# Where the gated layer's lead runs beside the last expert item: token sums on VectorE, splits directly behind them, block loads and sums earlier

## The chip, the cores and the metric

One core of a Trainium2 chip runs the whole program. The metric is device time in microseconds (us) of one execution, the median of several runs.

## What is computed

Attention output (3072 tokens of width 512) goes through a mixture of eight experts with one expert per token, and then through a gated layer:

```python
# experts: x [3072, 512], w1 [8, 512, 1024], w2 [8, 1024, 512]
for e in range(E):
    xe = x[expert_idx == e]
    h = np.maximum(xe @ w1[e], 0.0)
    out[expert_idx == e] = gate_w[expert_idx == e, None] * (h @ w2[e])
# gated layer: w_gate, w_val [512, 1536], w_out [1536, 512]
gate = 1.0 / (1.0 + np.exp(-(x @ w_gate)))
val = x @ w_val
return (gate * val @ w_out).astype(np.float32)
```

All of it is in float32.

## The kernel before

A float32 product is made of three TensorE products of rounded parts: each operand is split into a high part (a rounded copy, made on ScalarE, ACT) and a low part (the operand less the high part, made on VectorE, DVE), and high by high, high by low and low by high are added in PSUM.

**The experts** (`ffn`, `Moe`) run over nine items, each a group of tokens of one expert. An item has eight steps f = 0 to 7, one for each 128 of the 1024 hidden columns. A step has two groups of 12 matmuls: `mm1(i, f)`, L1101, here called *hidden product f*, whose result ACT and DVE turn into `hh` (L1105) and `hl` (L1106); and `mm2(i, f)`, L1118, here *output product f*, which needs `hh`, `hl` and the weights of the second layer. In the program the order within step f is: weight splits (`wh` on ACT, L999; `wl` on DVE, L1004), weight loads (L990), hidden product f + 1, then for the last item (i = 8, 352 tokens) `m2.lead(f)`, and then output product f. Each pair of weights serves two steps: the first layer's pair for hidden products 4 and 5 is split in step 2, the second layer's pair for output products 4 and 5 in step 3.

**The gated layer** (`Gated`) runs over four chunks of 768 tokens. For a chunk it multiplies 2 x 2 blocks with seven products instead of eight, so both operands need four sums of blocks besides the four blocks. A token operand is built twice, for u = 0 and 1: `yfetch` loads four blocks of 128 x 384 from `yT` with three DMAs (L1231 to L1233) into a tile `raw`, `ysum` adds four blocks (L1240), and `ysplit` splits blocks 1 to 4 (z = 0, 1536 columns) and 5 to 7 (z = 1, 1152 columns) into the tiles `yo` (L1246 on ACT, L1247 on DVE). A weight operand s = 0 to 11 is built in the same way: `afetch` (L1254), `asum` (L1265), `asplit` (L1279 on ACT, L1280 on DVE, into `set`), and `astore` (L1268) writes the blocks and sums out for the later chunks. `raw` has two buffers, so the load of a block waits for the split that last read its buffer. The products of set s are `first(s)` (L1331, seven products of six matmuls each).

`lead(f)` puts the first chunk's token operand and the first sets beside the last item's steps. Its last act, in step 7, is to start `first(0)`: two products X and Y of six matmuls each, which TensorE (PE) takes ahead of output product 7. The item before stores its result to `yT` (L1129) at the start of the last item, and the first `yfetch` waits for that store.

The order of instructions on every engine is the order in which the program issues them; nothing reorders them. The line that matters in `ffn` is the step's body:

```python
        if n + 1 < len(steps):
            mm1(*steps[n + 1])
...
            m2.lead(f)
        mm2(i, f)
```

Of the kernel before, what the change touches and what calls it, by code (L numbers as in the profile page):

```python
# [14 lines left out]
ALU = mybir.AluOpType  # L15
# [42 lines left out]
NSET = 2 * NJ  # L58
# [168 lines left out]
def graph():  # L227
# [12 lines left out]
    for t in range(NTILE):  # L240
# [15 lines left out]
        for s in (2 * t, 2 * t + 1):  # L256
# [4 lines left out]
            for j in range(4):  # L261
                first = [("NS", WIN if t else 128, s % 2)] if t < 2 and j == 0 else []
                add(
                    ("TTR", s, j), [("QK", s)] + first, [("QK", s, j - 2)] if j >= 2 else (),
                    cost=0.318 if i else 0.21,
                )
                add(
                    ("EXP", s, j), [("TTR", s, j)] + ([("PT", s - 3, 1)] if s >= 3 and j == 0 else []),
                    cost=0.38 if i else 0.293,
                )  # L270
# [937 lines left out]
class Gated:  # L1208
# [25 lines left out]
            out=x[:, 2:4, :].rearrange("p b n -> p (b n)"), in_=self.g.yT[(u + 2) * 128 : (u + 3) * 128, cols]  # L1234
        )

    def ysum(self, c, u):
        x = self.yr[c, u]
        for o, a, b in ((4, 0, 1), (6, 3, 0), (5, 3, 4), (7, 2, 5)):
            self.tc.nc.gpsimd.tensor_tensor(x[:, o, :], x[:, a, :], x[:, b, :], op=ALU.subtract)  # L1240

    def ysplit(self, c, u, z):
        x = self.yr[c, u]
# [93 lines left out]
    def first(self, s):  # L1337

        nc = self.tc.nc
        j, m = divmod(s % NSET, 2)  # L1340
        V, A, G = nc.vector, nc.scalar, nc.gpsimd
        last = s % NSET == NSET - 1
        X, Y, Z, W = (self.psum(b, f"q{b}")[:, :CH] for b in ((2, 3, 0, 1) if m else (6, 7, 4, 5)))
        u2 = self.tm.tile([128, CH], F32, tag="u2", name="u2", bufs=2)
        c, r = divmod(s, NSET)
        more = c + 1 < NCH
        if c == 0 and r < NSET - 2:
            self.asum(s + 2)
        if more and r >= NSET - 2:
            self.ysum(c + 1, r - NSET + 2)  # L1350
        self.product(X, 1, 0, s)
        A.activation(u2, X, AF.Copy)  # L1352
        self.product(Y, 4, 4, s)
        V.tensor_tensor(u2, Y, u2, op=ALU.add)  # L1354
        yield
        if last:
            self.hsplit(0, 0, 2)
        else:
            self.asplit(s + 1, 0)
        self.product(Z, 5, 5, s)  # L1360
        at = lambda half, tok: self.h[:, 2 * j + half, tok * CH : tok * CH + CH]
        dst = (lambda half, tok: self.g.op.tile([128, CH], F32, tag="t", name="t", bufs=3)) if m else at
        d22 = dst(1, 1)
        V.tensor_tensor(d22, Z, u2, op=ALU.add)
        if last:
            self.hsplit(0, 2, 4)
        else:
            self.asplit(s + 1, 1)
        if r < NSET - 3:
            self.afetch(s + 3)  # L1370
        elif more and r < NSET - 1:
            self.yfetch(c + 1, r - NSET + 3)
        if c == 0 and r < NSET - 2:
            self.astore(s + 2)
        if c == 0:
            if r in (3, 5):
                self.ofetch((r - 3) // 2)
            if r in (6, 8):
                self.osplit((r - 6) // 2, G)
            if r in (8, 10):  # L1380
                self.ofetch((r - 8) // 2 + 2)
        elif r in (2, 4, 6):
            self.oload(c, r // 2 - 1)
        self.product(W, 3, 3, s)
        V.tensor_tensor(d22, W, d22, op=ALU.add)  # L1385

        def gate(d, half, tok):
            if m:
                (V if last else G).tensor_tensor(at(half, tok), at(half, tok), d, op=ALU.mult)  # L1389
            else:  # L1390
                A.activation(d, d, AF.Sigmoid)

        gate(d22, 1, 1)
        self.product(X, 2, 1, s, False)
        if m:
            V.tensor_tensor(at(0, 0), X, at(0, 0), op=ALU.mult)  # L1396
        else:
            A.activation(at(0, 0), X, AF.Sigmoid)
        self.product(Z, 0, 6, s, False)
        d21 = dst(1, 0)  # L1400
        V.tensor_tensor(d21, Z, u2, op=ALU.add)
        gate(d21, 1, 0)
        self.product(W, 6, 2, s, False)
        d12 = dst(0, 1)
        V.tensor_tensor(d12, W, u2, op=ALU.add)
        gate(d12, 0, 1)
        yield
# [75 lines left out]

    def lead(self, f):

        if f < 2:
            self.yfetch(0, f)
        if f in (1, 2):
            self.ysum(0, f - 1)
        if 2 <= f < 6:  # L1490
            self.ysplit(0, f // 2 - 1, f % 2)
        if f == 3:
            sg = self.tm.tile([128, 1], F32, name="sg")
            self.tc.nc.scalar.activation(sg, self.g.nval[:, 0:1], AF.Sigmoid)
        if f in (4, 6):
            self.afetch(f // 2 - 2)
            if f == 6:
                self.astore(0)
            self.asum(f // 2 - 2)
        if f == 7:  # L1500
            self.afetch(2)
            self.astore(1)
            self.now = self.first(0)
            next(self.now)

# [435 lines left out]
```

## Time and profile before

| | |
|---|---|
| time, median of 3 runs (lowest to highest) | 1102.04 us (1101.3 to 1102.1) |
| the profiled execution's own time | 1103.0 us |
| its span in the trace | 1101.1 us |
| PE busy | 1028.4 us, 93% of the span |
| DVE busy | 829.0 us, 75% |
| ACT busy | 566.3 us, 51% |
| GpSimd (POOL) busy | 441.5 us, 40% |
| mean granted TensorE clock | 0.974 |

Busy time of an engine is the time in which it executes an instruction; the rest it waits. The last expert item lies at about 507 to 547 us of the span, and the first chunk of the gated layer begins there. In the views, a time in brackets at the end of a row is how long the engine was idle before that instruction, with what ended the idle time.

### The profile page before, as it was taken

To read this page: it belongs to the slowest core of one execution; us is meant where nothing else is said; L and a number is where in the kernel's file an instruction comes from. 1 tells how busy PE (TensorE), PEld (TensorE's weight loads), DVE (VectorE), ACT (ScalarE), POOL (GpSimd) and SP (SyncE) were. 2 spreads that over 40 slices of the span, in tenths; PEclk is the share of its full clock that TensorE was granted. 3 is DMA by queue.
4 is the path that set the end of the run, shared out by engine and by line. 5 is a ranking of instruction groups with operands and counts; after the bars stand their busy time and mean duration, and the time that the engine had idled before them with its cause. 6 is when DMAs were issued, how large, how long until landed. Compare 5 with 4: busy or idle time off the path is not lost.

```text
span 1101.1 us, 21478 instructions
## 1 busy us (share of the span) xinstructions
PE 1028.4 (93%) x7983; PEld 981.2 (89%) x7983; DVE 829.0 (75%) x1663; ACT 566.3 (51%) x1027; POOL 441.5 (40%) x612
## 2 busy tenths in 40 slices
PE   6987978788999999999899998999999999999994
PEld 5776767688889999999899998999999999999994
DVE  6987869655679778975767699666986679766782
ACT  6998979533344444544544464444534436444440
POOL 7998879730221222130878713214122250222102
PEclk9999989798999999999999999999999999999997
DMA  9899986477598899987568758663465725656061
GB/s 193 193 189 182 194 182 125 119 167 259 178 278 276 276 308 293 303 274 203 187 227 286 271 189 316 227 243 126 156 233 190 249 91 187 234 199 224 18 230 62
DMA packets 176216, 229.45 MB, mean 208 GB/s; under 512 B 90243, under 2 KB 140038, under 8 KB 172518
## 3 DMA queue, kind: packets, MB, share of 16 engines
q1 hardware_dynamic: 170566, 214.04, 64.6%
q0 software_dynamic: 5008, 13.93, 3.7%
q8 instruction: 65, 1.06, 0.4%
q14 instruction: 49, 0.40, 0.1%
q10 hardware_dynamic: 528, 0.02, 0.0%
HBM read 163.13 MB, written 60.51 MB: 203 GB/s over the span
## 4 chain that ended last, share of the span: by engine, by line
PE 71%; POOL 10%; DVE 6%; DMA 5%; issue 4%; ACT 2%; SPq 1%; another core or an unknown queue 0%; POOLq 0%; DVEq 0%; ACTq 0%
PE q L1331 30%; PE p L1429 14%; PE hp L1101 12%; PE acc L1118 12%; DMA vb<-vv 2%; POOL pl L597 1%; POOL xr L640 1%; PE mxt L1036 1%; POOL vv L484 1%; POOL lst L735 1%; DMA wr<-in_moe_w_dram 1%; DVE set L1321 1%; POOL ph L590 1%; DMA x<-xd,idx 1%; PE ptp L573 1%
## 5 line engine op out<-in xcount | busy, mean ns | idle before, releaser
L1331 PE MATMUL q<-yo,set 128*128 128x384 f32 x2016 | 354.5, 337 | 3.1 <-ACT set L1279 1.3
L1331 PEld LDWEIGHTS q<-yo,set 128*128 128x128 f32 x2016 | 348.6, 188 | 8.0 <-DVE h L1385 2.3
L1429 PE MATMUL p<-wy,set 128*128 128x256 f32 x1458 | 175.4, 281 | 5.0 <-DVE set L1321 4.1
L1429 PEld LDWEIGHTS p<-wy,set 128*128 128x128 f32 x1458 | 173.7, 189 | 6.6 <-DVE set L1321 5.1
L1101 PE MATMUL hp<-xT,wh 128*128 128x256 f32 (+7 forms) x576 | 147.3, 341 | 0.1
L1389 POOL TENSOR_TENSOR h<-h,t 128x384 f32<-128x384 f32 x60 | 60.6, 1018 | 164.2 <-DVE t L1385 160.6
L1280 DVE TENSOR_TENSOR set<-raw,set 128x1024 fp32r<-128x1024 f32 x96 | 110.6, 1154 | 2.3 <-ACT set L1279 2.3
L1101 PEld LDWEIGHTS hp<-xT,wh 128*128 128x128 f32 x576 | 101.9, 192 | 3.2 <-ACT wh L999 0.4
L1101 PE MATMUL hp<-xT,wl 128*128 128x256 f32 (+7 forms) x288 | 96.8, 336 | 1.1 <-DVE wl L1004 1.1
L1118 PE MATMUL acc<-hl,wh 128*128 128x256 f32 (+7 forms) x288 | 96.2, 334 | 0.4 <-DVE hl L1106 0.4
L1118 PE MATMUL acc<-hh,wh 128*128 128x256 f32 (+7 forms) x288 | 96.5, 335 | 0.0
L1118 PE MATMUL acc<-hh,wl 128*128 128x256 f32 (+7 forms) x288 | 96.1, 334 | 0.0
L1016 POOL DMA_INDIRECT x<-xd,idx x29 | 32.4, 1116 | 154.9 <-DMA idx<-lst 134.2
L1279 ACT ACTIVATE set<-raw 128x1024 fp32r<-128x1024 f32 x96 | 85.8, 944 | 15.3 <-PE p L1429 11.9
L1105 ACT ACTIVATE hh<-hp 128x256 fp32r<-128x256 f32 (+7 forms) x72 | 34.7, 482 | 113.3 <-PE hp L1101 110.2
L1004 DVE TENSOR_TENSOR wl<-wr,wh 128x1024 fp32r<-128x1024 f32 x64 | 80.9, 1266 | 13.2 <-ACT wh L999 11.8
L1352 ACT ACTIVATE u<-q 128x384 f32<-128x384 f32 x48 | 23.6, 492 | 122.1 <-PE q L1331 122.1
L1475 POOL DMA_INDIRECT out_dram<-o,idt x24 | 25.2, 1051 | 148.9 <-ACT set L1279 78.5
L1354 DVE TENSOR_TENSOR u<-q,u 128x384 f32<-128x384 f32 x48 | 26.8, 558 | 74.8 <-PE q L1331 73.3
L1320 ACT ACTIVATE set<-h 128x1152 fp32r<-128x1152 f32 (+1 forms) x60 | 62.8, 1098 | 37.7 <-DVE h L1396 16.4
L561 ACT ACTIVATE pp<-tt,mall 128x232 f32<-128x232 f32 (+1 forms) x192 | 79.8, 479 | 2.3 <-DVE mall L544 2.3
L1321 DVE TENSOR_TENSOR set<-h,set 128x1152 fp32r<-128x1152 f32 (+1 forms) x60 | 76.6, 1314 | 2.2 <-ACT set L1320 2.0
(204 smaller groups left out, 2142.7 us busy)
## 6 DMA issues: line engine op xcount, KB each, us to landing
wr<-in_moe_w_dram SPq DMA_DIRECT2D x64, 512.0 KB
raw<-us SPq DMA_DIRECT2D x36, 896.0 KB
wy<-wz SPq DMA_DIRECT2D x21, 1536.0 KB
us<-raw SPq DMA_DIRECT2D x12, 896.0 KB
wz<-wy SPq DMA_DIRECT2D x7, 1536.0 KB
kn<-in_k_dram SPq DMA_DIRECT2D x24, 256.0 KB
qn<-in_q_dram SPq DMA_DIRECT2D x24, 256.0 KB
vn<-in_v_dram SPq DMA_DIRECT2D x24, 256.0 KB
```

Source lines behind the costliest of these rows:

```text
L561: nc.scalar.activation(pp[s][:, j, 256 - w :], tt[s][:, j, :w], AF.Exp, bias=g.mall[:, t, h : h + 1], scale=-1.0)
L1004: self.tc.nc.vector.tensor_tensor(lo, self.raws.pop((z, p)), hi.bitcast(F32), op=ALU.subtract)
L1101: nc.tensor.matmul(bk, a[:, k, fs], b[:, k, :], start=(m == 0), stop=(m == 11))
L1105: nc.scalar.activation(hh, bk, AF.Relu)
L1118: nc.tensor.matmul(acc[i][dk], a[:, f % 2, d], b, start=(f == 0 and m == 0), stop=(f == NF - 1 and m == 2))
L1279: self.tc.nc.scalar.activation(h, x, AF.Copy)
L1280: self.tc.nc.vector.tensor_tensor(l, x, h.bitcast(F32), op=ALU.subtract)
L1320: self.tc.nc.scalar.activation(h, x, AF.Copy)
L1321: self.tc.nc.vector.tensor_tensor(l, x, h.bitcast(F32), op=ALU.subtract)
L1331: nc.tensor.matmul(bk, w[:, za, a, us], self.y[zy][:, y, u, :], start=(start and n == 0), stop=(n == 5), skip_group_check=not start,)
L1389: (V if last else G).tensor_tensor(at(half, tok), at(half, tok), d, op=ALU.mult)
L1429: nc.tensor.matmul(bks[t], w[:, za, j, 128 * t : 128 * t + 128], y[:, zy, j, :], start=(new and j == 0 and m == 0 and (end or t != 1)), st ...
```

## The change

The first chunk's token sums move from POOL to DVE; the sums of later chunks stay on POOL. Both token loads are issued in step 0 (before: steps 0 and 1). Steps 1 and 2 each do the sums of one half u and at once both of its splits (before: one split in each of steps 2 to 5). The loads and sums of sets 0 and 1 move from steps 4 and 6 to steps 3 and 4, and both stores to step 5 (before: steps 6 and 7).

```diff
-    def ysum(self, c, u):
+    def ysum(self, c, u, e):
         x = self.yr[c, u]
         for o, a, b in ((4, 0, 1), (6, 3, 0), (5, 3, 4), (7, 2, 5)):
-            self.tc.nc.gpsimd.tensor_tensor(x[:, o, :], x[:, a, :], x[:, b, :], op=ALU.subtract)
+            e.tensor_tensor(x[:, o, :], x[:, a, :], x[:, b, :], op=ALU.subtract)
...
         if more and r >= NSET - 2:
-            self.ysum(c + 1, r - NSET + 2)
+            self.ysum(c + 1, r - NSET + 2, G)
...
     def lead(self, f):
 
-        if f < 2:
-            self.yfetch(0, f)
+        if f == 0:
+            self.yfetch(0, 0)
+            self.yfetch(0, 1)
         if f in (1, 2):
-            self.ysum(0, f - 1)
-        if 2 <= f < 6:
-            self.ysplit(0, f // 2 - 1, f % 2)
+            self.ysum(0, f - 1, self.tc.nc.vector)
+            self.ysplit(0, f - 1, 0)
+            self.ysplit(0, f - 1, 1)
         if f == 3:
             sg = self.tm.tile([128, 1], F32, name="sg")
             self.tc.nc.scalar.activation(sg, self.g.nval[:, 0:1], AF.Sigmoid)
-        if f in (4, 6):
-            self.afetch(f // 2 - 2)
-            if f == 6:
-                self.astore(0)
-            self.asum(f // 2 - 2)
+        if f in (3, 4):
+            self.afetch(f - 3)
+            self.asum(f - 3)
+        if f == 5:
+            self.astore(0)
+            self.astore(1)
         if f == 7:
             self.afetch(2)
-            self.astore(1)
             self.now = self.first(0)
             next(self.now)
```

Its effect on the order, first on DVE, in steps 1 to 4 of the last item. `wl0` is the low part of first-layer weights, `wl1` of second-layer weights; `raw2_8773` is the token tile of u = 0 and `raw2_8816` (in the change `raw2_8777`) that of u = 1. Before:

```order
L1106 SCALAR_TENSOR_TENSOR hl_8813<-hp_8799,hh_8812 128x352
L1004 TENSOR_TENSOR wl0_8837<-wr0_8735,wh0_8836 128x1024
L1106 SCALAR_TENSOR_TENSOR hl_8856<-hp_8842,hh_8855 128x352
L1247 TENSOR_TENSOR yo1_8772<-raw2_8773,yo0_8771 128x4x384
L1004 TENSOR_TENSOR wl1_8878<-wr1_8797,wh1_8877 128x1024
L1106 SCALAR_TENSOR_TENSOR hl_8897<-hp_8883,hh_8896 128x352
L1247 TENSOR_TENSOR yo1_8772<-raw2_8773,yo0_8771 128x3x384
```

The same stretch on DVE in the change:

```order
L1106 SCALAR_TENSOR_TENSOR hl_8817<-hp_8803,hh_8816 128x352
L1240 TENSOR_TENSOR raw2_8773<-raw2_8773 128x384 x4
L1247 TENSOR_TENSOR yo1_8772<-raw2_8773,yo0_8771 128x4x384
L1247 TENSOR_TENSOR yo1_8772<-raw2_8773,yo0_8771 128x3x384
L1004 TENSOR_TENSOR wl0_8841<-wr0_8735,wh0_8840 128x1024
L1106 SCALAR_TENSOR_TENSOR hl_8860<-hp_8846,hh_8859 128x352
L1240 TENSOR_TENSOR raw2_8777<-raw2_8777 128x384 x4
L1247 TENSOR_TENSOR yo1_8772<-raw2_8777,yo0_8771 128x4x384
L1247 TENSOR_TENSOR yo1_8772<-raw2_8777,yo0_8771 128x3x384
L1004 TENSOR_TENSOR wl1_8884<-wr1_8801,wh1_8883 128x1024
L1106 SCALAR_TENSOR_TENSOR hl_8903<-hp_8889,hh_8902 128x352
```

The four sums and both splits of u = 0 now stand ahead of the weights `wl0` for hidden products 4 and 5 and of `hl` of step 3; those of u = 1 stand ahead of the weights `wl1` for output products 4 and 5 and of `hl` of step 4.

On the queue of loads and stores (SP), from the last item's step 0 on, as one piece of the difference:

```order
-L990 ISA
-L990 DMA wr_8797<-in_moe_w_dram 128x2x512
-L1231 DMA raw_8816<-yT 128x384
-L1232 DMA raw_8816<-yT 128x384
-L1233 DMA raw_8816<-yT 128x768
+L1231 DMA raw_8777<-yT 128x384
+L1232 DMA raw_8777<-yT 128x384
+L1233 DMA raw_8777<-yT 128x768
+L990 ISA
+L990 DMA wr_8801<-in_moe_w_dram 128x2x512
```

The loads of u = 1 pass one load of second-layer weights, the one for output products 4 and 5; the three loads of u = 0 stay where they were, ahead of both.

## Rows read from the trace of the kernel before

**Rows 1.** Chain of waits in time: start us, us, what; last expert item.
```profile
512.70 1.93 PE acc L1118 x12
...
519.63 6.17 DMA raw<-yT
```

**Rows 2.** PE in time, last item: start us, us, engine, line, op, [idle before].
```profile
522.23 0.48 PE L1101 MATMUL hp<-xT,wh 128*128 128x352 f32 x2
...
528.70 0.43 PE L1118 MATMUL acc<-hl,wh 128*128 128x352 f32 x1 [0.36 <-DVE hl L1106]
...
532.29 0.43 PE L1101 MATMUL hp<-xT,wl 128*128 128x352 f32 x1 [0.85 <-DVE wl L1004]
...
542.51 0.62 PE L1331 MATMUL q<-yo,set 128*128 128x384 f32 x2 [1.30 <-ACT set L1279]
543.87 0.96 PE L1331 MATMUL q<-yo,set 128*128 128x384 f32 x4 [0.74 <-DVE set L1280]
...
546.60 71.11 PE L1331 MATMUL q<-yo,set 128*128 128x384 f32 x396
```

**Rows 3.** POOL in time, last item.
```profile
520.57 1.02 POOL L1240 TENSOR_TENSOR raw<-raw 128x384 f32<-128x384 f32 x1 [29.92 <-PE hp L1101]
522.65 12.96 POOL L1240 TENSOR_TENSOR raw<-raw 128x384 f32<-128x384 f32 x7 [1.06 <-DMA raw<-yT]
535.57 6.01 POOL L1265 TENSOR_TENSOR raw<-raw 128x256 f32<-128x256 f32 x4
542.27 3.65 POOL L1265 TENSOR_TENSOR raw<-raw 128x256 f32<-128x256 f32 x4 [0.69 <-DMA raw<-up]
```

**Rows 4.** SP in time: issues of loads and stores, last item.
```profile
511.49 0.40 SPq L1129 DMA_DIRECT2D yT<-y  x1
...
516.05 1.49 SPq L1231 DMA_DIRECT2D raw<-yT  x1
...
530.31 8.59 SPq L1254 DMA_DIRECT2D raw<-up  x2
```

**Rows 5.** DVE in time, last item.
```profile
517.12 0.53 DVE L1106 SCALAR_TENSOR_TENSOR hl<-hp,hh 128x352 fp32r<-128x352 f32 x1 [1.71 <-ACT hh L1105]
518.85 1.22 DVE L1004 TENSOR_TENSOR wl<-wr,wh 128x1024 fp32r<-128x1024 f32 x1 [1.21 <-ACT wh L999]
...
524.21 2.04 DVE L1247 TENSOR_TENSOR yo<-raw,yo 128x1536 fp32r<-128x1536 f32 x1 [2.70 <-ACT yo L1246]
526.17 2.03 DVE L1004 TENSOR_TENSOR wl<-wr,wh 128x1024 fp32r<-128x1024 f32 x1
```

**Rows 6.** DVE groups by shape, 640 to 1100 us: xcount | busy us, mean ns.
```profile
L1247 DVE TENSOR_TENSOR yo<-raw,yo 128x1536 fp32r<-128x1536 f32 x6 | 10.5, 1748 | 0.0
...
L1247 DVE TENSOR_TENSOR yo<-raw,yo 128x1152 fp32r<-128x1152 f32 x6 | 8.1, 1348 | 0.0
...
L1389 DVE TENSOR_TENSOR h<-h,t 128x384 f32<-128x384 f32 x9 | 5.5, 608 | 0.3
```

**Rows 7.** ACT in time, last item.
```profile
522.68 1.49 ACT L1246 ACTIVATE yo<-raw 128x1536 fp32r<-128x1536 f32 x1 [1.73 <-DMA raw<-yT]
```

**Rows 8.** Stretches: from:to, length, busy PE, PEld, DVE, ACT, POOL, clock, DMA, GB/s.
```profile
546.60:635.20 88.60, 87.97 (x495) 84.79 (x494) 62.83 (x90) 39.05 (x63) 69.17 (x62) 1.00 0.76 267
...
952.60:1040.00 87.40, 87.40 (x507) 87.40 (x506) 58.77 (x93) 37.88 (x61) 18.25 (x18) 1.00 0.45 168
```

**Rows 9.** PE in time, end of the attention stage.
```profile
202.40 0.21 PE L614 MATMUL po<-vb,ph 128*128 128x65 f16 x1 [4.46 <-DMA vb<-vv]
```

**Rows 10.** Stretches about that wait, columns as in rows 8.
```profile
206.00:208.00 2.00, 2.00 (x15) 1.94 (x15) 2.00 (x7) 1.37 (x4) 2.00 (x3) 0.50 0.00 0
208.00:210.00 2.00, 1.20 (x25) 1.06 (x23) 2.00 (x2) 2.00 (x5) 1.92 (x2) 0.97 0.00 0
...
214.00:216.00 2.00, 1.96 (x11) 1.48 (x10) 1.65 (x6) 1.29 (x4) 1.83 (x5) 0.50 0.27 105
```

**Rows 11.** Chain of waits in time, first expert item at the half clock.
```profile
252.42 2.56 PE acc L1118 x12
```

## The prediction

> **What bounds the kernel now.** I read the page's busy shares first: TensorE is busy for 93% of the span, so only a change that alters TensorE's gaps can alter the time. Then I read the chain of waits through the last expert item. It runs over TensorE's groups of 12 matmuls, 1.93 us each [rows 1], leaves TensorE at the token load, follows the token and weight sums on POOL and the last split, and comes back to TensorE at 543.87 [rows 1 to 3]. TensorE in time shows what that costs. From the start of hidden product 4 (522.23) to the first product behind output product 7 (546.60) are 24.37 us [rows 2]. The work in it is nine groups of 12 matmuls, 9 x 1.93 = 17.37 us, and X and Y, twelve products of 384 columns at 87.40/507 = 0.172 us each [rows 8], 2.08 us: 19.45 us. **4.92 us are lost**, at four places: output product 4 waits for `hl`, hidden product 6 for `wl`, X and Y for the high and the low part of set 0 [rows 2]. The brackets there count idle time alone, 3.25 us; I go by starts. These 4.92 us are all that the change can win in this stretch. Behind it, the first chunk's products take 88.60 us and the last chunk's 87.40 [rows 8], so 1.2 us more lie there at most.
>
> **What the change does, step by step.** I set it on the clock of the trace before.
>
> 1. *The sums of u = 0 now wait on DVE.* DVE is through with `hl` of step 2 at 517.65 [rows 5], and its next instruction is the first sum. On POOL that sum began at 520.57 and the next one only at 522.65, when the third load had landed [rows 3]. The load can't come earlier: its issue at 516.05 stands behind the store of the item before, issued at 511.49 [rows 4], and the change alters nothing ahead of it. So DVE is held from 517.65 to 522.65. What is queued behind: both splits, the low weights for hidden products 4 and 5 (before at 518.85 [rows 5]) and `hl` of step 3.
>
> 2. *How long the block takes.* A sum of 128x384 on DVE lies between 0.53 us (the `hl` of 352 columns [rows 5]) and 1.02 us (the same sum on POOL [rows 3]); I take 0.61, DVE's operation of the same shape [rows 6]. Three sums are left at 522.65: 1.8 us, to 524.45. The low parts take 1.75 and 1.35 us [rows 6]; instructions in a row overlap a little, and I take 2.95 for both, to 527.4. With the weights' 1.22 [rows 5] this is 528.6. The high parts on ACT (1.49 for the larger [rows 7], about 1.2 for the smaller one, from 524.45) and the weights' high part behind them are done near 526.7, ahead of DVE.
>
> 3. *First new wait.* Hidden product 4 starts two matmuls at most (and those not before 526.7) and needs the low weights for its third, at 522.23 + 2 x 0.16 = 522.55. It gets them at 528.6: **6.05 us lost**, where nothing was lost before.
>
> 4. *The block of u = 1.* Its loads pass a load of weights on SP; they landed at 525.8 before [rows 1] and can land sooner, so nothing waits for them. The weights that they pass are not split before 532, so that costs nothing either. DVE does `hl` of step 3 to 529.05, four sums to 531.4, both low parts to 534.35, the low weights for output products 4 and 5 to 535.5 and `hl` of step 4 to 536.0. This is without POOL. But the first `raw` buffer is free at 527.4, so set 0 is loaded some 3 us earlier than the 530.31 of before [rows 4], and its four sums begin on POOL about 3.7 us behind the issue (the second of the pair of issues ended at 538.9 and its sums began at 542.27 [rows 3, 4]), at 531.1, for 3.65 to 6.0 us [rows 3]. Where POOL adds beside it, DVE's low part took 2.04 instead of 1.75 and the weights 2.03 instead of 1.22 [rows 5, 6]. The cost here lies between nothing and 1.5 us; I take 1.1, since three of these operations fall into the stretch, and `hl` of step 4 is done at 537.1.
>
> 5. *Second new wait.* TensorE, back at 528.6, has ten matmuls left of hidden product 4 (1.6 us) and two groups, so output product 4 would start its second matmul at 534.2. It gets `hl` at 537.15: **2.95 us lost**.
>
> 6. *What goes.* From there on everything has slack. The table load and the Sigmoid now stand behind `hh` of step 4 on ACT and put off the weights for hidden product 6 to 538.3, or 539.1 beside POOL, where they are needed at 539.2; this is what is late next. The sums of sets 0 and 1 end before 543, X is not before 546.6, and the last split of set 0 follows `hh` of step 7 to some 547.0, where Y needs it at 547.65. So the four waits of before go, 4.92 us.
>
> 7. *What costs nothing.* POOL has no other work until the sums of set 0. Both stores only wait on SP, ahead of nothing but the load of set 2, which waits for the split of set 0 in any case.
>
> **Sum:** 6.05 + 2.95 - 4.92 = **+4.1 us**. The profiled execution took 1103.0 us of its own (span 1101.1 and 1.9 around it), 1.0 above the median of 1102.04; so 1107.1 for such an execution and **1106.1 us** for the median.
>
> **The clock.** TensorE rests from 522.2 to 526.7. A rest of 4.46 us at the end of attention was followed by half the clock (1.2 of 2.4 GHz) until about 208, 5.7 us behind the restart at 202.40 [rows 9, 10]. If this comes here, the 34 matmuls up to output product 4 take 2.8 us longer, and it is reached at 537.0 instead of 534.2, still before `hl`. The second wait hides it, and the sum stays. This I expect.
>
> **The rivals.** A change can be told from no change here from about 0.2%, 2.2 us.
>
> *The clock stays low longer.* For: after 212 the profile shows half the clock although TensorE was 1.96 of 2.00 us busy [rows 10]. At half the clock a group of 256 columns takes 2.56 us [rows 11], so a matmul of 352 takes 2.56/12 x 352/256 = 0.293 us. From 528.6 the 34 matmuls then last until 538.6; if the clock is back only at 541, eight of output product 4 are done by then and four follow in 0.6 us: 541.6 instead of 538.9. That is +6.8 us, **1108.8**. Against: in rows 9 and 10 it was back after 5.7 us. By the Trainium skill (TensorE: Matmul & The Clock Gate, parts 1 and 4) sustained matmuls release the clock again and transposes count for less. By that rule the stretch after 212, where many instructions are transposes, says little of this one, and the sum stays at +4.1 against +6.8 by the row. No run here has shown yet which holds behind such a wait among products. The chance of this rival is 0.12.
>
> *POOL hardly collides, and the first chunk gains.* If set 0's sums fall beside DVE's waits, the 1.1 us go; if the sets' loads, now nearer to ready, spare the first chunk what it loses against the last one, 1.2 more go. This gives +1.8 us, **1103.9**, which counts as no change. For: POOL's sums beside TensorE's waits took only 3.65 us once [rows 3]. Against: the first chunk's loss recurs with its own stores and sums, which the change leaves. Chance 0.15.
>
> *Faster.* One place decides: the landing of the third load of u = 0. Each us that it comes sooner takes one off the first wait; the second wait moves with it. At 518.55 the sum is zero, and at 516.6 it is -2 us, **1100.1**. Against: the load was issued between 516.05 and 518.5 and first needs the store to land; nothing in the change speeds that up. Chance 0.05, general doubt about the order of the waits included.
>
> **How the numbers follow.** The forecast has 0.68: its own range goes from 1104.5 (no collision, sums a tenth of a us shorter) to 1107.7 (the largest collision and the slower sums). The whole range takes in the second rival and most of the first, 1103.2 to 1108.8. Slower by over 0.2% (above 1104.2): the forecast and the clock's rival, 0.80. Within 0.2%: the rival of the small loss, 0.15. Faster: 0.05.
>
> **What would show it.** Right: the four brackets of rows 2 are gone; TensorE waits 4 to 6 us at hidden product 4 for `wl` behind the token splits, then 1 to 3 us at output product 4 for `hl`; DVE sits idle before its first token sum until the third load; X and Y run without a wait, and the products behind output product 7 start near 550.7. Wrong: hidden product 4 starts on time, or the token loads land before 519; a granted clock below 1 beyond 536 would speak for the clock's rival; and if the first chunk's products took 87.4 us, for the small loss.

## The result and the profile after

| | before | after |
|---|---|---|
| median of 11 runs each, side by side (lowest to highest) | 1101.3 us (1096.42 to 1104.37) | 1106.91 us (1102.5 to 1113.33) |
| the profiled execution's own time | 1103.0 us | 1108.95 us |
| its span | 1101.1 us | 1107.0 us |
| PE busy | 1028.4 us | 1028.3 us |
| mean granted TensorE clock | 0.974 | 0.972 |

The ratio is 1.0055, with a 95% interval of 1.0032 to 1.0077: **slower, by 3.5 to 8.5 us**. The forecast was 1106.1 us, which is +4.1 on the earlier median of 1102.04; side by side the medians lie 5.6 us apart.

The executions of either kernel lie some 8 to 11 us apart, more than the effect, so two traces can't be compared by their spans. The changed kernel's trace already stands 3.92 us behind the other before the lead, in work that the change doesn't touch, and gains 1.8 us on it after the stretch measured here. What can be compared is the stretch of the prediction: from the time at which hidden product 4 would start without a wait (one matmul, 0.16 us, behind the start of the last matmul of output product 2) to the first product behind output product 7. The work in it is 19.45 us.

- before: 522.23 to 546.60, **24.37 us**, 4.92 lost;
- after: 526.15 to 554.26, **28.11 us**, 8.66 lost.

So the stretch costs 3.74 us more. PE in time, changed kernel:

```profile
530.49 0.95 PE L1101 MATMUL hp<-xT,wh 128*128 128x352 f32 x2 [4.19 <-ACT wh L999]
532.49 0.66 PE L1101 MATMUL hp<-xT,wl 128*128 128x352 f32 x1 [1.04 <-DVE wl L1004]
...
540.63 0.43 PE L1118 MATMUL acc<-hl,wh 128*128 128x352 f32 x1 [0.25 <-DVE hl L1106]
...
550.24 2.25 PE L1331 MATMUL q<-yo,set 128*128 128x384 f32 x12
...
554.26 2.07 PE L1331 MATMUL q<-yo,set 128*128 128x384 f32 x11
```

The four brackets of [rows 2] are gone: X and Y are one row of twelve products without a wait. In their place hidden product 4 waits, and its third matmul starts at 532.49 instead of 526.47. Output product 4 waits only shortly. DVE in time, same kernel:

```profile
521.04 0.52 DVE L1106 SCALAR_TENSOR_TENSOR hl<-hp,hh 128x352 fp32r<-128x352 f32 x1 [1.71 <-ACT hh L1105]
524.34 0.56 DVE L1240 TENSOR_TENSOR raw<-raw 128x384 f32<-128x384 f32 x1 [2.78 <-DMA raw<-yT]
526.67 1.62 DVE L1240 TENSOR_TENSOR raw<-raw 128x384 f32<-128x384 f32 x3 [1.77 <-DMA raw<-yT]
528.27 3.03 DVE L1247 TENSOR_TENSOR yo<-raw,yo 128x1536 fp32r<-128x1536 f32 x2
531.22 1.22 DVE L1004 TENSOR_TENSOR wl<-wr,wh 128x1024 fp32r<-128x1024 f32 x1
...
532.78 2.08 DVE L1240 TENSOR_TENSOR raw<-raw 128x384 f32<-128x384 f32 x4
534.89 3.57 DVE L1247 TENSOR_TENSOR yo<-raw,yo 128x1536 fp32r<-128x1536 f32 x2
538.38 1.76 DVE L1004 TENSOR_TENSOR wl<-wr,wh 128x1024 fp32r<-128x1024 f32 x1
540.06 0.51 DVE L1106 SCALAR_TENSOR_TENSOR hl<-hp,hh 128x352 fp32r<-128x352 f32 x1
```

Behind `hl` of step 2 (to 521.56) DVE is held for the token loads until 526.67, apart from one sum; then three sums, two splits and the weights follow in one piece, to 532.44, and the third matmul starts. That is the first wait. The second piece is the same work for u = 1, but slower (3.57 and 1.76 us for what took 3.03 and 1.22), while POOL adds beside it:

```profile
535.54 10.77 POOL L1265 TENSOR_TENSOR raw<-raw 128x256 f32<-128x256 f32 x8 [40.99 <-DMA raw<-up]
```

Four stretches of 4 us show the clock (the column after the five engines) and the load of the DMA engines (the next one):

```profile
526.00:530.00 4.00, 0.30 (x2) 0.01 (x1) 3.29 (x5) 3.16 (x3) 0.00 (x0) 1.00 0.97 328
530.00:534.00 4.00, 2.46 (x7) 2.01 (x8) 4.00 (x7) 1.42 (x3) 0.00 (x0) 0.52 0.87 284
534.00:538.00 4.00, 4.00 (x19) 4.00 (x18) 3.94 (x4) 3.94 (x5) 2.46 (x2) 0.63 0.11 40
538.00:542.00 4.00, 3.75 (x23) 3.46 (x23) 4.00 (x5) 3.23 (x5) 3.92 (x3) 1.00 0.38 131
```

TensorE comes back at half the clock (1.2 GHz); its matmuls are 0.29 us apart until about 536.8, and 0.16 from there on.

### The profile page after: what moved, and what is told of

Its sections match the earlier page's. It is cut to its first block, busy times and chain, and to the rows that moved or that the text cites. A ratio compares the mean times of both kernels' runs of the same rounds, so it can differ in the third digit from the quotient of the medians.

```text
span 1107.0 us, 21474 instructions
## 1 busy us (share of the span) xinstructions
PE 1028.3 (93%) x7983; PEld 983.1 (89%) x7983; DVE 830.6 (75%) x1671; ACT 564.9 (51%) x1027; POOL 432.5 (39%) x604
## 4 chain that ended last, share of the span: by engine, by line
PE 73%; POOL 8%; DVE 6%; DMA 5%; issue 3%; ACT 2%; SPq 1%; POOLq 0%; DVEq 0%; ACTq 0%
PE q L1331 30%; PE p L1429 14%; PE acc L1118 12%; PE hp L1101 12%; DMA vb<-vv 2%; DMA lst<-idall,si 1%; POOL xr L640 1%; POOL pl L597 1%; PE mxt L1036 1%; POOL lst L735 1%; POOL vv L484 1%; PE ptp L573 1%; POOL vv L478 1%; DVE set L1321 1%; DMA x<-xd,idx 1%
## 5 line engine op out<-in xcount | busy, mean ns | idle before, releaser
L1429 PE MATMUL p<-wy,set 128*128 128x256 f32 x1458 | 175.2, 281 | 5.1 <-DVE set L1321 4.0
L1429 PEld LDWEIGHTS p<-wy,set 128*128 128x128 f32 x1458 | 173.6, 189 | 6.5 <-DVE set L1321 4.8
L1265 POOL TENSOR_TENSOR raw<-raw 128x256 f32<-128x256 f32 x48 | 56.3, 1193 | 59.0 <-DMA raw<-up 53.3
```

What stands on the lines that cost most here:

```text
L1429: nc.tensor.matmul(bks[t], w[:, za, j, 128 * t : 128 * t + 128], y[:, zy, j, :], start=(new and j == 0 and m == 0 and (end or t != 1)), st ...
```

## The experiments

Each kernel has one profile, from which the stretch is taken, and 9 to 12 runs beside the kernel before on the same chip (there 1112.7 to 1112.9 us, for e12 1098.8). The interval of a ratio is some 3 us wide to either side, so the stretch decides, and the ratio only says whether it fits. One trace each does not show how far a stretch varies by itself; three kernels that the theory takes as equal (the change, e5 and e6) lie 0.3 us apart. Behind the stretch the first chunk took between 87.9 us (e10) and 90.0 (e9), with 88.6 before and in the change; why was not tried, and it is more than the last five stretches differ by.

| kernel | stretch, us | lost in it (e5 and e12 with their added products) | ratio to before (95%) |
|---|---|---|---|
| before | 24.37 | 4.92 | |
| the change | 28.11 | 8.66 | 1.0055 (1.0032 to 1.0077) |
| e2_sums_on_pool | 30.97 | 11.52 | 1.0061 (1.0031 to 1.0092) |
| e6_sets_back | 27.80 | 8.35 | 1.0041 (1.0017 to 1.0064) |
| e5_clock_held | 27.94 | 8.49 | 1.0024 (1.0001 to 1.0048) |
| e4_other_source | 27.57 | 8.12 | 1.0044 (1.0012 to 1.0076) |
| e8_load_first | 24.97 | 5.52 | 1.0037 (1.0009 to 1.0065) |
| e3_one_step_later | 28.94 | 9.49 | 1.0053 (1.0023 to 1.0083) |
| e7_splits_back | 26.09 | 6.64 | 1.0019 (0.9992 to 1.0045) |
| e1_half_sums | 24.01 | 4.56 | 0.9983 (0.9953 to 1.0014) |
| e9_spread | 24.19 | 4.74 | 1.0021 (0.9993 to 1.0048) |
| e10_spread_early_table | 24.71 | 5.26 | 1.0013 (0.9985 to 1.0042) |
| e11_table_early | 24.34 | 4.89 | 1.0003 (0.9971 to 1.0035) |
| e12_spread_clock | 25.52 | 6.07 | 1.0016 (0.9989 to 1.0044) |

The theory: the added wait is DVE's block of token sums and splits, held first by the landing of the token loads. Its rivals: the move of the sums to DVE is itself the loss; the half clock is; the earlier loads of the sets are.

### Which part of the change costs the time

**e2_sums_on_pool** is the change with the first chunk's sums back on POOL:

```diff
-            self.ysum(0, f - 1, self.tc.nc.vector)
+            self.ysum(0, f - 1, self.tc.nc.gpsimd)
```

> The change with its token sums given back to POOL; loads, splits at once and the rest stay. My theory (the splits in steps 1 and 2 hold the weights back, whoever adds): hidden product 4 still waits, 6 to 7 us, since the second high part waits for POOL's last sum at about 525.7 on the clock of before; the stretch is 27.5 to 29.5 us, against 28.1 with the change. Rival (the sums on DVE are the cost): the stretch falls back to some 24 to 25 us.

PE and POOL in time:

```profile
545.65 0.95 PE L1101 MATMUL hp<-xT,wh 128*128 128x352 f32 x2 [6.70 <-ACT wh L999]
548.57 0.66 PE L1101 MATMUL hp<-xT,wl 128*128 128x352 f32 x1 [1.97 <-DVE wl L1004]
```
```profile
539.04 10.35 POOL L1240 TENSOR_TENSOR raw<-raw 128x384 f32<-128x384 f32 x7 [0.74 <-DMA raw<-yT]
```

The wait at hidden product 4 grows: seven sums took 10.35 us on POOL. The stretch of 30.97 us is above what was expected, and 2.86 above the change. So the move of the sums to DVE is not the loss; in the new order of the splits, it saves 2.9 us.

**e6_sets_back** is the change with the loads, sums and stores of the sets in the steps of before:

```diff
-        if f in (3, 4):
-            self.afetch(f - 3)
-            self.asum(f - 3)
-        if f == 5:
-            self.astore(0)
-            self.astore(1)
+        if f in (4, 6):
+            self.afetch(f // 2 - 2)
+            if f == 6:
+                self.astore(0)
+            self.asum(f // 2 - 2)
         if f == 7:
             self.afetch(2)
+            self.astore(1)
```

> The change with set 0's and set 1's loads, sums and stores put back to the steps where the kernel before has them; token sums and splits stay as changed. Theory: this part of the change does nothing by itself, since GpSimd and the queue come to the sets' loads only when the token buffers come free: stretch 27.8 to 28.4 us, as the change's 28.11. Rival: the earlier loads of the sets cost a collision (1.1 us of VectorE's time beside GpSimd's sums), which goes: 27.0 us or less.

27.80 us, as the theory had it, with POOL's eight sums again beside DVE's second block (10.74 us). Moving the sets is worth 0.3 us here, which one trace each can't tell from nothing; their loads come when a token buffer is free.

**e7_splits_back** is the change with the sums on DVE in steps 1 and 2, but each split back in its own step:

```diff
         if f in (1, 2):
             self.ysum(0, f - 1, self.tc.nc.vector)
-            self.ysplit(0, f - 1, 0)
-            self.ysplit(0, f - 1, 1)
+        if 2 <= f < 6:
+            self.ysplit(0, f // 2 - 1, f % 2)
```

> The change with its splits back in steps 2 to 5; the sums stay on DVE in steps 1 and 2 and so still wait there for the token load. This parts the wait for the load from the length of the block. My theory: hidden product 4 waits for its low weights only until the load, three sums and the weights are done, some 3 us instead of 6; TensorE rests too short for the clock to fall; small waits at output product 4, hidden product 6 and Y; the stretch is 23.5 to 25.5 us. Rival (the wait for the load is nearly the whole loss): 27 us or more.

```profile
536.18 0.66 PE L1101 MATMUL hp<-xT,wl 128*128 128x352 f32 x1 [3.04 <-DVE wl L1004]
```
```profile
534.00:538.00 4.00, 1.82 (x6) 1.82 (x7) 3.93 (x7) 1.99 (x2) 0.00 (x0) 0.68 1.00 355
538.00:542.00 4.00, 4.00 (x16) 4.00 (x15) 4.00 (x5) 2.40 (x3) 0.00 (x0) 0.50 0.14 53
```

The first wait is cut to 3.20 us (536.18 instead of 532.98), 2.82 us less, about the 3.03 us of the two splits that no longer stand ahead, and the second is gone. The stretch misses the expected range by 0.6 us, since the clock fell even behind this shorter rest. The 22 matmuls to the end of output product 3 then took 6.39 us instead of 3.53: 2.86 us, which no second wait hides here.

### What holds the first sum

**e4_other_source** loads the first chunk's token blocks from another tensor (the chunk's output is of other data), so that no load has to wait for the store of the item before:

```diff
+        if c == 0:
+            k = self.g.up32[0, 0].rearrange("h p c -> p h c")
+            self.tc.nc.sync.dma_start(out=x[:, 1, :], in_=k[:, 0, 0:CH])
...
+            return
         k = self.g.yT[u * 128 : (u + 1) * 128, cols]
```

> The change, but the first chunk's token blocks are loaded from the prepared weights instead of the item results, so that the first token load doesn't wait for the store of the item before (the first chunk's output is that of other data). My theory: the loads land some 4 us earlier, the wait at hidden product 4 falls from 6 us to 1.5 to 3 us, and the stretch is 24 to 25.5 us, near that of before. Rival (DVE's work in the block is the whole loss): the stretch stays above 27 us.

A miss: 27.57 us. SP and DVE in time:

```profile
525.78 0.40 SPq L1129 DMA_DIRECT2D yT<-y  x1
...
526.86 1.18 SPq L1198 DMA_DIRECT2D idt<-ids  x1
528.13 3.71 SPq L1232 DMA_DIRECT2D raw<-up  x1
```
```profile
534.67 0.56 DVE L1248 TENSOR_TENSOR raw<-raw 128x384 f32<-128x384 f32 x1 [2.74 <-DMA raw<-up]
536.50 1.62 DVE L1248 TENSOR_TENSOR raw<-raw 128x384 f32<-128x384 f32 x3 [1.27 <-DMA raw<-up]
```

The load is issued at once, but the issue itself takes 3.71 us behind the store, the weights and a small load (`idt`), and the third load lands only half a us sooner against hidden product 4 than in the change (0.02 us ahead of its nominal start, there 0.52 behind). The dependency on the store was not what set the landing. In the trace the transfers of this queue land in the order of their issue: store 530.28, weights 532.04, `idt` 533.56, token loads 534.08, 534.58 and 536.47. What drew out the issue is not settled: the view of waits puts 2.8 us of it down to a hidden product on TensorE, and the trace can't part that from the transfers ahead.

**e8_load_first** therefore also issues the token loads ahead of that store (the chunk's output is again of other data):

```diff
-            nc.sync.dma_start(
+            put = lambda: nc.sync.dma_start(
                 out=g.yT.rearrange("(k p) n -> p k n", p=128)[:, :, ds(g.oreg[r] + c0, n)], in_=y
             )
+            if i == NIT - 2:
+                held.append(put)
+            else:
+                put()
...
             m2.lead(f)
+            while held:
+                held.pop()()
```

> As the kernel with the token blocks from the prepared weights, but with the loads issued ahead of the store of the item before, so that they don't stand behind its traffic either (the first chunk's output is that of other data). My theory: the loads land before DVE is through with hl of step 2, DVE isn't held, hidden product 4 waits 1 to 2 us and output product 4 some 2 to 3 us; the stretch is 22.5 to 25 us. Rival (the block's length alone): 27 us or more.

SP, DVE and PE in time:

```profile
514.32 0.45 SPq L1203 DMA_DIRECT2D idt<-ids  x1
515.16 4.65 SPq L1239 DMA_DIRECT2D raw<-up  x1
```
```profile
527.83 2.08 DVE L1255 TENSOR_TENSOR raw<-raw 128x384 f32<-128x384 f32 x4
```
```profile
534.16 0.43 PE L1102 MATMUL hp<-xT,wl 128*128 128x352 f32 x1 [1.18 <-DVE wl L1004]
...
542.29 0.43 PE L1119 MATMUL acc<-hl,wh 128*128 128x352 f32 x1 [2.26 <-DVE hl L1107]
```
```profile
542.00:546.00 4.00, 3.71 (x16) 3.71 (x17) 3.15 (x4) 0.80 (x1) 3.92 (x4) 0.67 0.55 221
```

The four sums start right behind `hl` of step 2 (to 527.92). The first wait is 1.34 us and the second 2.41, in the order of the change. So the hold was worth 4.7 us of the first wait; the rest of it is the block's own length. What ended the hold is the earlier place in the queue: in the change SP waits 9.0 us for the store's data before it comes to the loads, and here their issue ends 8.0 us earlier against hidden product 4. That the store's own traffic was the hold is not shown; the first issue takes 4.65 us here with no such store ahead. The stretch falls by 3.14 only, because now the clock fell behind the second wait, where nothing hides it (1.66 us: 0.76 in output product 4 and 0.90 in hidden product 6). The first chunk took 0.8 us longer than in the kernel before, so the trace explains 1.4 us of the time; the ratio's interval begins at 1.0 us (1.0009).

**e3_one_step_later** gives the loads time in another way, by the same blocks in steps 2 and 3:

```diff
-        if f in (1, 2):
-            self.ysum(0, f - 1, self.tc.nc.vector)
-            self.ysplit(0, f - 1, 0)
-            self.ysplit(0, f - 1, 1)
+        if f in (2, 3):
+            self.ysum(0, f - 2, self.tc.nc.vector)
+            self.ysplit(0, f - 2, 0)
+            self.ysplit(0, f - 2, 1)
```

> The change with its sums and splits moved from steps 1 and 2 to steps 2 and 3. If the wait of DVE for the token load is a large part of the loss, hidden product 4 starts on time and the loss moves: about 1 us at output product 4 and 4 to 5.5 us at hidden product 6, whose weights now stand behind the block of u = 1; the stretch is 25 to 26.5 us. Rival (the size of the block alone decides): the waits move by a step and add up to the same 9 us or so, 28 us.

```profile
542.97 0.43 PE L1118 MATMUL acc<-hl,wh 128*128 128x352 f32 x1 [0.92 <-DVE hl L1106]
...
548.62 0.59 PE L1101 MATMUL hp<-xT,wh 128*128 128x352 f32 x2 [3.62 <-ACT wh L999]
550.64 0.66 PE L1101 MATMUL hp<-xT,wl 128*128 128x352 f32 x1 [1.43 <-DVE wl L1004]
```

The rival was right. Hidden product 4 starts on time, but the blocks now hold the weights of hidden product 6: 5.5 us lost there, 1.35 at output product 4, and 2.5 at the half clock. The block as a whole is too long for one step, wherever it stands.

### What the half clock costs

**e5_clock_held** is the change with 36 products of no use in the first rest, so that TensorE never rests there:

```diff
         mm2(i, f)
+        if i == NIT - 1 and f == 2:
+            bk = g.ps.tile([128, 512], F32, tag="b7", name="dm")[:, 0:352]
+            wh = wts[0, (i * NF + 2) // 2][0]
+            for m in range(36):
+                nc.tensor.matmul(
+                    bk, wh[:, m % 4, 0:128], xT[i][0][:, m % 4, :], start=(m == 0), stop=(m == 35)
+                )
```

> The change with 36 matmuls of 352 columns added ahead of hidden product 4, into a PSUM bank that nothing reads, 36 x 0.161 = 5.8 us at the full clock: they fill the rest of TensorE that was followed by the half clock. My theory (the half clock is hidden by the second wait, DVE decides): the clock stays at 1.00, output product 4 now waits some 2.5 us for hl instead of 0.4, and the stretch stays at 27.7 to 28.5 us. Rival (the clock is part of the loss): about 2 us less, 26 us.

```profile
550.12 0.43 PE L1118 MATMUL acc<-hl,wh 128*128 128x352 f32 x1 [2.25 <-DVE hl L1106]
```
```profile
548.00:552.00 4.00, 1.88 (x12) 1.88 (x13) 4.00 (x5) 2.61 (x5) 3.86 (x4) 1.00 0.40 131
```

The clock stayed at 1.00 throughout, and the stretch is 27.94 instead of 28.11: the second wait is back at 2.41 us (550.12 instead of 547.71), since `hl` comes no sooner. So in the change the half clock costs no more than the 0.17 us between the two; the second wait hides it.

### Orders that might beat both

**e1_half_sums** keeps the order of before and moves only the sums of u = 0 to DVE, in step 2:

```diff
-        if f in (1, 2):
-            self.ysum(0, f - 1)
+        if f == 2:
+            self.ysum(0, 0, self.tc.nc.vector)
+            self.ysum(0, 1, self.tc.nc.gpsimd)
```

> The order of before, with one thing of the change kept: the sums of u = 0 go to DVE, in step 2, where they stand behind the weights for hidden products 4 and 5 and behind hl of step 3; the sums of u = 1 stay on POOL and can begin as soon as their loads land. I measure the stretch from the nominal start of hidden product 4 to the first product behind output product 7: 24.4 us before, 28.1 us with the change. My theory (the place of the block on DVE decides, not the engine of the sums): no wait at hidden product 4; POOL reaches the sums of set 0 some 2 us earlier, so the waits at X and Y shrink from 2.8 us to under 1 and the stretch is 21.5 to 23 us, about 2 us faster than before. Rival (token sums on DVE cost in themselves, because DVE lacks 2 us per half): 25 us or more.

```profile
539.36 8.56 POOL L1240 TENSOR_TENSOR raw<-raw 128x384 f32<-128x384 f32 x4 [35.97 <-DVE yo L1247]
```

A miss: 24.01 us. POOL started its four sums of u = 1 only at 539.36. The row names a split on DVE that ended then, but the sums stand ahead of that split in the program, and the second of their loads had landed only at 539.20; the loads held them. POOL then took 2.14 us for each, beside DVE, where the kernel before shows 1.02 for one [rows 3] while DVE had only an `hl` to do. So the sums of set 0 came only 0.4 us sooner against hidden product 4, and Y waited as before.

**e9_spread** puts all sums on DVE and gives every block a step of its own: sums in steps 2 and 4, splits in 3 and 5. The token loads go back to steps 0 and 1, the store of set 1 to step 7 (not shown).

```diff
-        if f in (1, 2):
-            self.ysum(0, f - 1, self.tc.nc.vector)
-            self.ysplit(0, f - 1, 0)
-            self.ysplit(0, f - 1, 1)
+        if f in (2, 4):
+            self.ysum(0, f // 2 - 1, self.tc.nc.vector)
+        if f in (3, 5):
+            self.ysplit(0, f // 2 - 1, 0)
+            self.ysplit(0, f // 2 - 1, 1)
...
-        if f in (3, 4):
-            self.afetch(f - 3)
-            self.asum(f - 3)
+        if f in (3, 5):
+            self.afetch(f // 2 - 1)
+            self.asum(f // 2 - 1)
```

> A version made from what the runs so far show: all token sums on DVE, away from POOL, but spread: sums of u = 0 in step 2, its splits in step 3, sums of u = 1 in step 4, its splits in step 5, so that no step's weights and hl wait behind more than 3 us of other work; the loads of set 0 in step 3 and of set 1 in step 5. If the place and not the engine decides: no wait at hidden product 4, at output product 4 under 0.5 us, at hidden product 6 under 1 us, some 1 to 2 us in all at X and Y; the stretch is 21 to 23 us, 1.5 to 3 us faster than before. Rival (any sums on DVE cost more than they give): 25 us or more.

ACT in time:

```profile
538.11 1.06 ACT L999 ACTIVATE wh<-wr 128x1024 fp32r<-128x1024 f32 x1 [3.82 <-DMA wr<-in_moe_w_dram]
...
541.98 1.28 ACT L1495 ACT_TABLE_LOAD   x1
543.27 0.20 ACT L1495 ACTIVATE sg<-nval 128x1 f32<-128x1 f32 x1
543.38 1.04 ACT L999 ACTIVATE wh<-wr 128x1024 fp32r<-128x1024 f32 x1
```

24.19 us, a miss again. The waits of the change are gone, and X and Y lose 0.9 us instead of 2.8. But hidden product 6 lost 2.1 us: its weights stand on ACT behind both high parts, which themselves stood behind a late load of weights, and behind the table load; 1.65 us of half clock followed. Two edits take this up.

**e10_spread_early_table** loads the table in step 2 and splits u = 0 in steps 2 and 3 (shown against e9_spread):

```diff
-        if f == 3:
+        if f == 2:
             sg = self.tm.tile([128, 1], F32, name="sg")
             self.tc.nc.scalar.activation(sg, self.g.nval[:, 0:1], AF.Sigmoid)
...
-        if f in (3, 5):
-            self.ysplit(0, f // 2 - 1, 0)
-            self.ysplit(0, f // 2 - 1, 1)
+        if f in (2, 3):
+            self.ysplit(0, 0, f - 2)
+        if f == 5:
+            self.ysplit(0, 1, 0)
+            self.ysplit(0, 1, 1)
```

> The spread order (sums on VectorE in steps 2 and 4, every block behind another step's high and low part) with two edits: the table load and the Sigmoid moved from step 3 to step 2, and the high part of u = 0 taken in step 2, its low part in step 3. Theory: the 2 us that the spread order lost at hidden product 6 came from ScalarE's queue, where the weights stood behind the table load (1.28 us) and a late weight load; with the table load ahead of it most of that goes. Stretch 21.5 to 23.2 us, against 24.37 for the kernel before; time 0 to 2 us under the kernel before. Rival: the weights' high part waits for its load alone, and the wait stays; stretch 24 us or more.

```profile
542.20 0.43 PE L1101 MATMUL hp<-xT,wl 128*128 128x352 f32 x1 [0.52 <-DVE wl L1004]
...
551.47 0.97 PE L1331 MATMUL q<-yo,set 128*128 128x384 f32 x4 [1.27 <-DVE set L1280]
552.94 0.62 PE L1331 MATMUL q<-yo,set 128*128 128x384 f32 x2 [0.50 <-ACT set L1279]
```
```profile
546.06 3.68 DVE L1247 TENSOR_TENSOR yo<-raw,yo 128x1536 fp32r<-128x1536 f32 x2
549.66 1.75 DVE L1280 TENSOR_TENSOR set<-raw,set 128x1024 fp32r<-128x1024 f32 x1
```

The theory's step held and its sum did not: hidden product 6 lost 0.78 us instead of 2.1, but X and Y now lost 3.6, and output product 7 behind them 0.9. X waited for the low part of set 0, which stood on DVE behind both splits of u = 1; Y waited for POOL, whose four sums for set 0 began 11.0 us behind the nominal start of hidden product 4 and took 7.52 us beside DVE's sums and splits.

**e12_spread_clock** is the spread order with eight products of no use ahead of hidden product 6 (shown against e9_spread):

```diff
         mm2(i, f)
+        if i == NIT - 1 and f == 4:
...
+            for m in range(8):
+                nc.tensor.matmul(
+                    bk, wh[:, m % 4, 0:128], xT[i][0][:, m % 4, :], start=(m == 0), stop=(m == 7)
+                )
```

> The spread order with eight products of no use (352 columns, 0.16 us each) ahead of hidden product 6, where the spread order waits 1.2 us for ScalarE's weights and 0.9 us for the low part, and then ran 1.65 us longer at half the clock. Theory: the clock's fall is what keeps the spread order from gaining; with TensorE's rest cut to under 1 us the clock stays at 1.00, and the stretch is 22.3 to 23.0 us, against 24.37 for the kernel before; time 1 to 2.5 us under the kernel before. Rival: the clock falls all the same, or the filled rest was what the loads needed; stretch 24.0 us or more.

```profile
529.00:533.00 4.00, 3.33 (x20) 3.04 (x21) 3.97 (x7) 2.06 (x4) 0.71 (x1) 1.00 0.42 131
...
541.00:545.00 4.00, 4.00 (x18) 4.00 (x18) 1.24 (x3) 0.95 (x2) 2.08 (x3) 0.64 0.73 290
```
```profile
534.57 3.67 DVE L1254 TENSOR_TENSOR yo<-raw,yo 128x1536 fp32r<-128x1536 f32 x2
538.16 1.74 DVE L1287 TENSOR_TENSOR set<-raw,set 128x1024 fp32r<-128x1024 f32 x1
```

At hidden product 6 the clock stayed at 1.00 and nothing was lost beside the waits. Yet the stretch is 25.52 us: X then waited 1.94 us for the low part of set 0, and the clock fell there. The rival's number came, though by neither of its reasons. The low part stood on DVE behind both splits of u = 1; X did not wait for POOL here, and ACT had the high part by 535.92. So DVE's own order is the next bound, and time won ahead of it is waited for at X.

**e11_table_early** moves only the table load, in the kernel before, from step 3 to step 2:

```diff
+        if f == 2:
+            sg = self.tm.tile([128, 1], F32, name="sg")
+            self.tc.nc.scalar.activation(sg, self.g.nval[:, 0:1], AF.Sigmoid)
         if f in (1, 2):
             self.ysum(0, f - 1)
...
-        if f == 3:
-            sg = self.tm.tile([128, 1], F32, name="sg")
-            self.tc.nc.scalar.activation(sg, self.g.nval[:, 0:1], AF.Sigmoid)
```

> The kernel before with one edit: the table load and the Sigmoid in step 2 instead of step 3. Theory: the wait of 0.85 us at hidden product 6 goes for the most part, since ScalarE's high part of those weights no longer stands behind the table load; the waits of X and Y stay, because GpSimd's sums set them. Stretch 23.5 to 24.0 us. Rival: that wait is VectorE's own, and the stretch stays at 24.3 to 24.5 us. The time can't be told from the kernel before in either case.

DVE in time:

```profile
543.64 1.73 DVE L1247 TENSOR_TENSOR yo<-raw,yo 128x1152 fp32r<-128x1152 f32 x1
545.29 2.04 DVE L1004 TENSOR_TENSOR wl<-wr,wh 128x1024 fp32r<-128x1024 f32 x1
```

The theory did not hold: 24.34 us. The low weights for hidden product 6 have no wait for ACT ahead of them; they wait for DVE, which has a split in front, and take 2.04 us beside POOL instead of 1.22.

None of the five can be told from the kernel before by its time.

## Why the prediction was right

By its own steps, times of the trace after less 3.92 us:

1. *DVE held.* Predicted from 517.65 to 522.65; measured from 517.64 to 522.75. Right in size. One reason was wrong: it said that the load "first needs the store to land". e4 took that need away and the landing hardly moved; e8, which also put the loads ahead of the store in the queue, ended the hold.
2. *Length of the block.* Predicted to be through at 528.6; measured 528.52. e8 and e7 each took one part of the wait away: the hold 4.7 us, the two splits 2.8 (6.02 against 3.20). Together that is more than 6.02, so the parts are not a sum: without both, the weights would be early.
3. *First wait.* 6.05 predicted, 6.02 measured.
4. *Second block and POOL.* `hl` of step 4 at 537.1 predicted, 536.65 measured. The slowing by POOL, taken as 1.1 us, was 0.54 at the splits and 0.54 at the weights, 1.08; in e7, where POOL is idle in these steps, the second split and the weights take 1.35 and 1.22 us. By the Trainium skill (SBUF — State Buffer, "SBUF: two separate sides") VectorE and GpSimd share a pair of ports that one instruction holds at a time while the other is blocked. The traces agree that both are held up, DVE's weights from 1.22 to 1.76 us and POOL's sum from 1.02 to 2.14 (e1); that either is blocked for a whole instruction they do not show.
5. *Second wait.* 2.95 predicted. Of it 0.42 us showed as a wait, less than the 1 to 3 us that the prediction gave as its sign, and 2.1 were the half clock: the 35 matmuls from 532.49 to where output product 4 was due took 7.72 us instead of 5.62. The paragraph on the clock had said that a wait hides it; e5 shows it.
6. *What goes.* All four waits, 4.92 us, as predicted. One reading was off: before, X ran through (539.82 to 541.21), and the waits for both parts of set 0 stood within Y.
7. *What costs nothing.* The sets' loads: e6.

The sum was +4.1 us; the stretch gives +3.74, since `hl` of step 4 came 0.45 us sooner than forecast. The measured median is 0.8 us above the forecast of 1106.1. That it lies so near is in part luck: the median of the kernel before was 0.7 us lower than the one the forecast started from, and of the 5.6 us between the medians the stretch shows 3.74. The other 1.9 us are within the interval (3.5 to 8.5) and in no part of the argument.

**The rivals.** *The clock stays low longer* did not come: it was back at 536.8, 4.3 us behind 532.49, with nothing but products in between. By the Trainium skill (TensorE: Matmul & The Clock Gate, part 1) sustained matmuls release it again; the trace agrees. *The small loss* did not come either: POOL did collide, and the first chunk took as long as before, 88.62 us against 88.58 from the end of the stretch to its first product of L1429. *Faster* named the right place: with the loads early (e8) the loss shrinks to +0.6 us. By the prediction's own steps it would have been -0.3 (a first wait of 1.7, the second of 2.95, less 4.92): DVE is not free before 517.65, so its -2 us for a landing at 516.6 could not come. Between -0.3 and +0.6 stands the half clock behind the second wait (1.66 us), which the prediction counted as hidden; the two waits were 0.9 us shorter.

**What stays open.** Why the executions differ by 8 to 11 us was not tried, nor what draws out the issue of the first token load (e4, e8). Nor was an order tried that spreads DVE's blocks and also has set 0's sums and its low part done sooner.

## What to carry to other kernels

When work moves to an engine that runs strictly in order, ask first when its data lands: everything behind the first instruction waits with it, so put it behind the small results that TensorE needs soon, and let no block be longer than one step. A faster engine shortens the block (here by 2.9 us) but not its wait for a transfer, and taking away a transfer's dependency did not help while it kept its place in the queue. Look also at what the next bound is before counting the waits that an order removes; here every order that took one away met the next.

## What was not expected of the hardware

- **The clock fell behind shorter rests than forecast.** The prediction knew a rest of 4.46 us [rows 9]. Here half the clock also came behind an idle time of 3.04 us (e7), of 2.26 (e8) and of 1.04 and 0.67 together (e9), and cost 2.86, 1.66 and 1.65 us; it came behind 1.76 us in e12 too. It did not come behind 2.25 us in e5, nor behind 1.30 and 0.74 in the kernel before. So a wait of 2 us can cost nearly twice its length; what decides whether it does was not settled.
- **An issue on the queue can itself take 3.7 us** (e4: 3.71 us where the same issue took 1.49 in the kernel before [rows 4]; e8: 4.65). The view of waits names a product on TensorE for 2.8 of the 3.71 us; whether that or the transfers ahead held it was not tried.
- **A sum on POOL took twice as long beside a working DVE**: 8.56 us for four in e1, where one took 1.02 beside a single `hl` [rows 3], and DVE's own instructions are slowed too.
